# One core, attention and MLP of a decode step: three blocks of the output weights loaded mid-run in eight-row transfers, and w2 in four parts

## The chip, the cores and the metric

The kernel runs on one core of a Trainium2 chip. The metric is the time of one execution on the device in microseconds; the time before is 1313.02 us, the median of three runs (1312.48 to 1313.17). All arrays are float32.

## The reference

For eight tokens (B = 8, one position each, D = 512), with `xn = layernorm(x)`:

```
q  = (xn @ wq) as 32 heads of 128
k, v = the cached keys and values of 8 heads, 8192 positions, each serving 4 query heads
o  = softmax(q k^T / sqrt(128)) v                    (per token and head)
A  = o (8 x 4096) @ wo (4096 x 512)
h  = xn @ w1 + b1  (512 -> 1792);  act = h * tanh(softplus(h))
out = x + A + act @ w2  (1792 -> 512)
```

The caches are by far the largest part: 8 x 8 x 8192 x 128 numbers each for keys and values, 268 MB each. wq and wo have 8.4 MB each, w1 and w2 3.7 MB each.

## The kernel before

The host lays the arrays out so that every load is contiguous rows. The attention is worked through in 32 *units* j, each one token b = j % 8 and one pair m = j // 8 of key-value heads. A unit needs one key load and one value load, each 128 rows (partitions) of 64 KB, 8.39 MB (`load_unit`, L119 to L127).

One large buffer `kv` holds a value load and two key loads that overlap by half (L55 to L59). So a new key load can only be issued when the first half of the scores of the unit before has been computed (L446 to L450), and a new value load when the matmuls on the former one are done (L456 to L458). A second buffer `ws` takes a quarter of wq (2 MB) four times, each for the next eight units (L114 to L117). All these loads are issued on SyncE's queue (SP); x and b1 alone are loaded from ScalarE's queue (L132 and L134), x in 8 rows of 2 KB, b1 in 4 rows of 1792 B.

The schedule is written by hand: each engine runs the operations in the order of the program, and a framework adds the semaphores. A step of the loop (L441 to L472) for unit j is, in this order:

- `scores`: 32 products of the unit's keys with the spread queries into PSUM `S` (64 instructions, L279), with the issue of the next key load between the two halves.
- `softmax` (L289 to L313): maximum, transposed to and fro by TensorE, the exponential into the work tile `e` by ScalarE (L310).
- `values(j - 1)` (L337 to L354): 32 products of the *former* unit's weights with its values (64 instructions, L341), then four VectorE instructions that fold the result into `os` (L349, L351). After its matmuls the value load of unit j is issued.
- `key_weights(j + 1)` (two VectorE products, L262), and once in eight units `load_q`, `project` (products of wq on TensorE into PSUM `H`, copied into a tile that shares its name and buffers with `e`) and `spread`.
- `turn` (L315 to L334): TensorE permutes `e` into PSUM `X`, VectorE transposes and sums it into `pt8`, the weights of the next `values`.
- `merge(j - 1)` (L356 to L359): one product that turns `os`, scaled into `oT`, which holds the attention's result as 128 rows (position in the head) by head and token.

In the first unit `mish` computes the hidden layer and leaves its activations in `aT`. So w2's product could be done at any time; only its place in the buffer sets when w2 is loaded.

After the loop come the tail's loads (L475 to L487), all in `kv`: wo in four transfers of 2 MB (each with four *blocks* u of 128 rows by 4 KB), then w2 in three parts of 2, 1 and 0.5 MB. The tail's work in program order: `values` of the last unit, `outputs` (L409 to L419) for m = 0, 1, 2, eight products each, which accumulate o @ wo in PSUM `A` as four groups of partitions by head; `merge` of the last unit; `outputs` for m = 3; a copy of `A` by ScalarE (L495); `down` (L421 to L431) with w2's first part into PSUM `H`; four products with `bsel` that add the four groups of `A` into `H` (L497 to L504); `down` with the other parts; the addition of x by VectorE (L508) and the store (L509).

Of the kernel before, what the change touches and what calls it, by code (L numbers as in the profile page):

```python
# [8 lines left out]
F32 = mybir.dt.float32  # L9
# [4 lines left out]
P = 128  # L14
B = 8
D = 512
HKV = 8
REP = 4
DH = 128
# [8 lines left out]
BW = 1024  # L28
CC = D // P
# [3 lines left out]
Q = P // G  # L33
# [15 lines left out]
NJ = PL * HALF  # L49

W2R = 7

# [13 lines left out]
def kernel(  # L66
# [12 lines left out]
    nc = tc.nc  # L79
# [8 lines left out]
    ws = const.tile([P, CC * BW], F32, name="ws")  # L88
# [124 lines left out]
    def project():  # L213

        w = ws.rearrange("p (c f) -> p c f", c=CC)
        for d in range(2):
            for c in range(CC):
                nc.tensor.matmul(  # L218
                    H[Q * c : Q * c + B, :],
                    xn4[:, c, :],  # L220
                    w[:, c, d * 512 : (d + 1) * 512],
                    start=True,
                    stop=True,
                )
            qp = work.tile([P, 512], F32, name="e")
# [12 lines left out]
        return qT  # L238
# [50 lines left out]
    def softmax(j):  # L289
        nm = work.tile([P, 1], F32, name="nm")  # L290
        nc.vector.tensor_reduce(nm, S, axis=AX.X, op=ALU.max, negate=True)  # L291
        nc.tensor.transpose(M[:1, 0:P], nm, ident)  # L292
        nr = work.tile([1, 2, REP], F32, name="nr")
        row = M[:1, 0:P].rearrange("p (c d k h) -> p d h c k", c=2, d=2, h=REP)
        for d in range(2):
            nc.vector.tensor_reduce(nr[:, d], row[:, d], axis=AX.XY, op=ALU.min)
        nx = work.tile([1, 2, 2, NH * G, REP], F32, name="nx", bufs=1)
        for c in range(2):
            nc.vector.tensor_copy(  # L299
                nx[:, c],  # L300
                nr.rearrange("p d (o h) -> p d o h", o=1).to_broadcast([1, 2, NH * G, REP]),
            )
# [12 lines left out]
    def turn(j, lsel):  # L315
        e = E.pop(j)
        for g in range(4):
            nc.tensor.matmul(X[:, g], perm[:, g], e, start=True, stop=True)  # L318
        nc.tensor.matmul(M[:, 136 : 136 + H2], ones, lsel, start=True, stop=True)  # L319
        RT[j] = work.tile([P, H2], F32, name="rt", bufs=3)  # L320
        nc.vector.reciprocal(RT[j], M[:, 136 : 136 + H2])  # L321
        for tl in range(TL):
            nc.vector.transpose(  # L323
                tr.rearrange("p (l t) c -> p t l c", t=TL)[:, tl],
                X.rearrange("p g (t q l) -> p t l g q", t=TL, q=PP)[:, tl],
            )
        for d in range(2):
            half = slice(64 * d, 64 * (d + 1))
            nc.vector.tensor_reduce(  # L329
                pt8[half, :, :, d * REP : (d + 1) * REP].rearrange("p c y h -> p y c h"),  # L330
                tr[half].rearrange("p y (g c h) -> p y c h g", g=4, c=HALF),
                axis=AX.X,
                op=ALU.add,
            )  # L334


    def values(j, vt):  # L337
        for n in range(NJ):
            l, c = divmod(n, HALF)
            q = n % G  # L340
            nc.tensor.matmul(  # L341
                O[Q * q : Q * (q + 1), :],
                pt8[:, c, TL * l : TL * (l + 1), :].rearrange("p t h -> p (t h)"),
                vt[:, 512 * n : 512 * (n + 1)],
                start=(n < G),
                stop=(n >= NJ - G),
            )
        os = work.tile([P, DH], F32, name="os")
# [55 lines left out]
        nc.vector.tensor_copy(aT, turned.rearrange("p (j q) -> p j q", q=Q)[:, :, :B])  # L404


    A = X[:, 0]

    def outputs(m, t):  # L409
        w = t.rearrange("p (u f) -> p u f", u=4)  # L410
        for d in range(2):
            for h in range(REP):
                nc.tensor.matmul(
                    A[Q * h : Q * h + B, :],
                    oT[:, m, d * REP + h, :],
                    w[:, d * 2 + h // 2, h % 2 * D : (h % 2 + 1) * D],
                    start=(m == 0 and d == 0),
                    stop=(m == NP - 1 and d == 1),
                )  # L419

    def down(lo, hi, w):  # L421
        for j in range(2 * lo, 2 * hi):
            for g in range(G):
                at = (j - 2 * lo) * D + g * P
                nc.tensor.matmul(  # L425
                    H[Q * g : Q * g + B, :P],
                    aT[:, j, :],
                    w[:, at : at + P],
                    start=(j == 0),
                    stop=(j == 2 * W2R - 1),  # L430
                )  # L431

# [8 lines left out]
    for j in range(UNITS):  # L441
        b = j % B
        more = j // B + 1 < NP

        k = k_t.pop(j)
        scores(j, k, j % 2 == 1, 0)  # L446
        if j == UNITS - 1:
            v_t[j] = load_unit(v, j, K_AT[0])
        elif j > 0:
            k_t[j + 1] = load_unit(kT, j + 1, K_AT[(j + 1) % 2])  # L450
        scores(j, k, j % 2 == 0, 1)
        WK.pop(j)
        lsel = softmax(j)
        os = None
        if j > 0:
            os = values(j - 1, v_t.pop(j - 1))  # L456
        if j + 1 < UNITS:
            v_t[j] = load_unit(v, j, V_AT)  # L458
            if more and b == SPREAD_Q:
                spread(qT)  # L460
            key_weights(j + 1)
        if j == 0:
            mish(w1_t, b1_sb, kv[:, W1_AT : W1_AT + 6 * FG])
        if more and b == LOAD_Q:
            load_q(j // B + 1)
        if more and b == MAKE_Q:
            qT = project()
        turn(j, lsel)
        if j > 0:
            merge(j - 1, os)  # L470
        if more and b == SPREAD_Q - 1:
            selections()  # L472


    w_o = [kv[:, 4096 * m : 4096 * (m + 1)] for m in range(NP)]  # L475
    for m in range(NP):
        nc.sync.dma_start(
            w_o[m].rearrange("p (u f) -> p u f", u=4),
            wo[4 * m : 4 * (m + 1)].rearrange("u p f -> p u f"),
        )  # L480
    w2_rows = w2.rearrange("j p f -> (j p) f").rearrange("(q i) f -> q (i f)", i=W2R)
    w2_t = []
    parts = ((0, 4), (4, 6), (6, 7))
    for lo, hi in parts:
        t = kv[:, W2_AT + lo * BW : W2_AT + hi * BW]
        nc.sync.dma_start(t, w2_rows[:, lo * BW : hi * BW])
# [4 lines left out]
        outputs(m, w_o[m])  # L491
    merge(UNITS - 1, os)
    outputs(NP - 1, w_o[NP - 1])
    a_sb = work.tile([P, 512], F32, name="e")
    nc.scalar.copy(a_sb, A)  # L495
    down(*parts[0], w2_t[0])
    for g in range(G):  # L497
        nc.tensor.matmul(
            H[Q * g : Q * g + B, :P],
            bsel[:, :B],  # L500
            a_sb[:, g * P : (g + 1) * P],
            start=False,
            stop=False,
        )  # L504
    for p, t in zip(parts[1:], w2_t[1:]):
        down(*p, t)
    res = work.tile([P, DH], F32, name="os")
    nc.vector.tensor_add(res, H[:, :P], xres)  # L508
    nc.sync.dma_start(out, res)  # L509


# [36 lines left out]
```

## Time and profile before

| what | value |
|---|---|
| median of three runs | 1313.02 us (1312.48 to 1313.17) |
| the profiled execution, and its span | 1313.46 us, 1311.7 us |
| granted TensorE clock, mean | 0.877 |
| bytes read from HBM | 561.01 MB, 428 GB/s over the span |
| value loads, key loads | 32 each, median 30.1 and 29.9 us from issue to landing |
| wo transfers in the tail | 4 of 2048 KB, median 24.5 us to landing |
| w2 parts in the tail | 2048, 1024 and 512 KB; 35.4, 20.7 and 20.5 us to landing |

The span runs from the first to the last instruction; the execution's time is a little longer. "Share" of DMA is the mean busy share of the core's sixteen DMA engines; within short windows it can pass 1 by some per cent. In the rows of a window, each engine's busy time is followed by a count of instructions in brackets; the last three numbers are the granted TensorE clock, the DMA share and GB/s. A matmul on float32 shows as two instructions. "<-" in square brackets names what ended the engine's idle time.

### The profile page before, as it was taken

The page shows a single profiled execution, that of the slowest core. Times are in us where ns is not written, and L with a number is a line of the kernel's source. Part 1 is how long each engine was busy: PE and PEld are TensorE (multiplying, and loading weights), DVE is VectorE, ACT ScalarE, POOL GpSimd, SP SyncE. Part 2 cuts the span into 40 slices and gives each one's busy share as a digit, 9 for nine tenths or more (in the row PEclk, how much of TensorE's full clock was granted, in tenths as well). Part 3 has the DMA queues.
Part 4 walks back from the last instruction along what each step waited for, and adds up shares of the span by engine and source line. Part 5 has one row for each costly group of instructions (what it writes and reads, how often), then busy time and mean ns, then how long its engine had stood idle before and what let it go on. Part 6 is the DMA issues. An engine that isn't in the chain of part 4 may idle for free.

```text
span 1311.7 us, 11148 instructions
## 1 busy us (share of the span) xinstructions
PE 985.5 (75%) x5040; PEld 341.1 (26%) x5040; DVE 515.0 (39%) x728; ACT 40.2 (3%) x88; POOL 2.2 (0%) x9
## 2 busy tenths in 40 slices
PE   5968877768877668777878777687687678677666
PEld 3322222222322222222322222232232222222222
DVE  3463344432444442334243344414444432344431
ACT  1000000000000000000000000000000000000000
POOL 0000000000000000000000000000000000000000
PEclk9989888888888888887888788788898888888898
DMA  9999999999999999999999999999999999999997
GB/s 393 450 422 439 428 434 431 430 444 428 432 432 434 428 440 424 440 426 434 432 428 446 416 442 430 430 440 422 438 430 436 430 430 432 436 424 438 426 418 313
DMA packets 13591, 561.79 MB, mean 428 GB/s; under 512 B 1244, under 2 KB 1376, under 8 KB 4584
## 3 DMA queue, kind: packets, MB, share of 16 engines
q1 hardware_dynamic: 13520, 561.06, 99.2%
q8 instruction: 39, 0.64, 0.2%
q14 instruction: 8, 0.07, 0.0%
q10 hardware_dynamic: 24, 0.02, 0.0%
HBM read 561.01 MB, written 0.07 MB: 428 GB/s over the span
## 4 chain that ended last, share of the span: by engine, by line
DMA 73%; PE 23%; DVE 2%; issue 0%; ACT 0%; SPq 0%; DVEq 0%
DMA kv<-in_v 71%; PE o L341 20%; DMA kv<-in_w 3%; PE s L279 1%; DVE pt L329 1%; PE x L244 1%; PE h L425 0%; PE m L229 0%; PE h L218 0%; PE h L370 0%; DVE kv L392 0%; DVE tr L323 0%; DVE wk L262 0%; DVE nm L291 0%; ACT L177 0%
## 5 line engine op out<-in xcount | busy, mean ns | idle before, releaser
L279 PE MATMUL s<-kv,wk 128*64 128x512 f32 x2048 | 503.3, 654 | 179.3 <-DMA kv<-in_kT 175.4
L341 PE MATMUL o<-kv,pt 128*32 128x512 f32 x2048 | 269.9, 687 | 56.0 <-DMA kv<-in_v 46.4
L279 PEld LDWEIGHTS s<-kv,wk 128*64 128x64 f32 x2048 | 156.4, 151 | 500.9 <-issue 318.7
L329 DVE TENSOR_REDUCE pt<-tr 64x512 f32<-64x2048 f32 x64 | 241.3, 3770 | 1.6
L291 DVE TENSOR_REDUCE nm<-s 128x1 f32<-128x512 f32 x32 | 22.1, 691 | 369.2 <-PE s L279 369.2
L341 PEld LDWEIGHTS o<-kv,pt 128*32 128x32 f32 x2048 | 70.1, 124 | 229.4 <-issue 170.7
L318 PE MATMUL x<-e,perm 128*128 128x512 f32 x256 | 125.8, 636 | 2.0 <-ACT qr L251 2.0
L349 DVE TENSOR_SCALAR os<-o,isel 128x128 f32<-128x128 f32 x32 | 11.2, 351 | 277.3 <-PE o L341 277.3
L323 DVE STREAM_TRANSPOSE tr<-x 128x512 f32<-128x512 f32 x128 | 78.6, 671 | 0.0
L262 DVE TENSOR_TENSOR wk<-qr,mask 128x512 f32<-128x512 f32 x64 | 62.9, 1026 | 19.8 <-ACT qr L251 19.8
L318 PEld LDWEIGHTS x<-e,perm 128*128 128x128 f32 x256 | 49.0, 202 | 74.5 <-issue 72.0
L310 ACT ACTIVATE e<-s,nmx 128x512 f32<-128x512 f32 x32 | 22.0, 687 | 1097.4 <-DVE nmx L307 1097.4
L351 DVE SCALAR_TENSOR_TENSOR os<-o,isel,os 128x128 f32<-128x128 f32 x96 | 33.7, 351 | 3.4
L292 PE MATMUL m<-ident,nm 128*1 128x128 f32 x32 | 8.7, 273 | 28.8 <-DVE nm L291 28.8
L303 PE MATMUL m<-ident,nx 1*128 1x1 f32 x32 | 7.0, 219 | 24.2 <-DVE nx L299 24.2
L244 PE MATMUL x<-qT,tr 128*128 128x64 f32 x128 | 19.3, 315 | 3.0 <-ACT qr L251 2.7
L244 PEld LDWEIGHTS x<-qT,tr 128*128 128x128 f32 x128 | 18.1, 226 | 6.2 <-ACT qr L251 3.3
L321 DVE RECIPROCAL rt<-m 128x8 f32<-128x8 f32 x32 | 6.6, 207 | 33.4 <-PE m L319 33.4
L358 PE MATMUL m<-hsel,os 128*128 128x8 f32 x64 | 12.4, 266 | 9.3 <-DVE rt L321 9.3
L312 DVE TENSOR_SCALAR lsel<-rsel,l 128x8 f32<-128x8 f32 x32 | 7.4, 231 | 30.1 <-ACT e L310 30.1
L292 PEld LDWEIGHTS m<-ident,nm 128*1 128x1 f32 x32 | 2.5, 79 | 57.0 <-DVE nm L291 57.0
L319 PEld LDWEIGHTS m<-lsel,ones 128*128 128x128 f32 x64 | 12.2, 190 | 15.4 <-issue 15.2
(88 smaller groups left out, 163.7 us busy)
## 6 DMA issues: line engine op xcount, KB each, us to landing
ws<-in_wq SPq DMA_DIRECT2D x4, 2048.0 KB, 35.9
kv<-in_wo SPq DMA_DIRECT2D x4, 2048.0 KB, 24.5
kv<-in_w SPq DMA_DIRECT2D x1, 3584.0 KB, 26.7
kv<-in_w SPq DMA_DIRECT2D x1, 2048.0 KB, 35.4
kv<-in_w SPq DMA_DIRECT2D x1, 1024.0 KB, 20.7
kv<-in_kT SPq DMA_DIRECT2D x32, 29.9
kv<-in_v SPq DMA_DIRECT2D x32, 30.1
kv<-in_w SPq DMA_DIRECT2D x1, 512.0 KB, 20.5
```

Of the source, the lines that this page charges most:

```text
L244: nc.tensor.matmul(X[:, half, k * 64 : (k + 1) * 64], wide[:, half * 8 + k], qT, start=True, stop=True,)
L262: nc.vector.tensor_mul(w[:, :, d], q[:, :, d].to_broadcast([P, DI, NH * G, REP]), mask[:, d * NH * G : (d + 1) * NH * G] .rearrange("p (o ...
L279: nc.tensor.matmul(S[64 * c : 64 * (c + 1), :], w[:, i].rearrange("p d k h -> p (d k h)"), kk[:, i, c, :], start=(part == 0 and n == 0), s ...
L291: nc.vector.tensor_reduce(nm, S, axis=AX.X, op=ALU.max, negate=True)
L310: nc.scalar.activation(e, S, AF.Exp, bias=nmx, accum_out=l)
L318: nc.tensor.matmul(X[:, g], perm[:, g], e, start=True, stop=True)
L319: nc.tensor.matmul(M[:, 136 : 136 + H2], ones, lsel, start=True, stop=True)
L323: nc.vector.transpose(tr.rearrange("p (l t) c -> p t l c", t=TL)[:, tl], X.rearrange("p g (t q l) -> p t l g q", t=TL, q=PP)[:, tl],)
L329: nc.vector.tensor_reduce(pt8[half, :, :, d * REP : (d + 1) * REP].rearrange("p c y h -> p y c h"), tr[half].rearrange("p y (g c h) -> p y ...
L341: nc.tensor.matmul(O[Q * q : Q * (q + 1), :], pt8[:, c, TL * l : TL * (l + 1), :].rearrange("p t h -> p (t h)"), vt[:, 512 * n : 512 * (n ...
L351: nc.vector.scalar_tensor_tensor(os, O[:, DH * i : DH * (i + 1)], isel[:, i : i + 1], os, op0=ALU.mult, op1=ALU.add)
L358: nc.tensor.matmul(M[:, 168 : 168 + H2], os, hsel, start=True, stop=True)
```

## The change

Three edits, which belong together:

- **Three blocks of wo mid-run.** In units 22, 24 and 26, right behind the value load, one block of wo (block 0, 1 or 2; 512 KB) is loaded into `ws`, which wq no longer needs after unit 21. The block goes to partitions 0 to 31 as rows of 16 KB (four of its 128 rows side by side), in four transfers of eight partitions each: r, r + 4, ..., r + 28. In the following unit its eight products on 32 rows are added into PSUM `H` ahead of `turn`. For that, `turn_o` once brings the needed part of `oT` into the same order (four products with columns of the identity, one VectorE copy into `oX`). The tail's first transfer of wo has one block instead of four, and `outputs(0)` two products instead of eight.
- **w2 in four parts** of 1, 1, 1 and 0.5 MB in place of 2, 1 and 0.5.
- **The sum of wo ahead of w2.** wo's products accumulate in `H` through the run; in the tail the copy and the four `bsel` products come first, into PSUM `O`, and all of w2's products after them.

With these go: `project` stands behind `turn` instead of ahead of it, and the tiles `e` and `os` have one buffer each instead of two.

```diff
+FEW = 32
+LOAD_O = (22, 24, 26)
...
+    oX = const.tile([FEW, CC, 2 * len(LOAD_O) * B], F32, name="oX")
...
-        e = E[j] = work.tile([P, 512], F32, name="e")
+        e = E[j] = work.tile([P, 512], F32, name="e", bufs=1)
...
+    def load_o(u):
+
+        rows = wo[u].rearrange("(e r i) f -> r e (i f)", r=4, i=CC)
+        for r in range(4):
+            nc.sync.dma_start(ws[r:FEW:4], rows[r])
+
+    def turn_o():
+
+        n = 2 * len(LOAD_O) * B
+        o = oT[:, 0].rearrange("p h b -> p (h b)")[:, :n]
+        for i in range(CC):
+            nc.tensor.matmul(
+                M[:FEW, 256 + i * n : 256 + (i + 1) * n], ident[:, i::CC], o, start=True, stop=True
+            )
+        nc.vector.tensor_copy(oX.rearrange("p i n -> p (i n)"), M[:FEW, 256 : 256 + CC * n])
+
+    def early(u):
+        for n in range(2):
+            for i in range(CC):
+                nc.tensor.matmul(
+                    H[Q * i : Q * i + B, :],
+                    oX[:, i, (2 * u + n) * B : (2 * u + n + 1) * B],
+                    ws[:FEW, i * BW + n * D : i * BW + (n + 1) * D],
+                    start=(u == 0 and n == 0),
+                    stop=False,
+                )
...
+                u = d * 2 + h // 2
+                if m == 0 and u < len(LOAD_O):
+                    continue
                 nc.tensor.matmul(
-                    A[Q * h : Q * h + B, :],
+                    H[Q * h : Q * h + B, :],
...
+        if j in LOAD_O:
+            load_o(LOAD_O.index(j))
+        if j - 1 in LOAD_O:
+            if j - 1 == LOAD_O[0]:
+                turn_o()
+            early(LOAD_O.index(j - 1))
+        turn(j, lsel)
         if more and b == MAKE_Q:
             qT = project()
-        turn(j, lsel)
...
     for m in range(NP):
+        lo = len(LOAD_O) if m == 0 else 0
         nc.sync.dma_start(
-            w_o[m].rearrange("p (u f) -> p u f", u=4),
-            wo[4 * m : 4 * (m + 1)].rearrange("u p f -> p u f"),
+            w_o[m].rearrange("p (u f) -> p u f", u=4)[:, lo:],
+            wo[4 * m + lo : 4 * (m + 1)].rearrange("u p f -> p u f"),
         )
...
-    parts = ((0, 4), (4, 6), (6, 7))
+    parts = ((0, 2), (2, 4), (4, 6), (6, 7))
...
-    nc.scalar.copy(a_sb, A)
-    down(*parts[0], w2_t[0])
+    nc.scalar.copy(a_sb, H)
     for g in range(G):
         nc.tensor.matmul(
-            H[Q * g : Q * g + B, :P],
+            O[Q * g : Q * g + B, :P],
             bsel[:, :B],
             a_sb[:, g * P : (g + 1) * P],
-            start=False,
+            start=True,
             stop=False,
         )
-    for p, t in zip(parts[1:], w2_t[1:]):
+    for p, t in zip(parts, w2_t):
         down(*p, t)
```

More of the change, by code (lines that the diff above doesn't have):

```diff
@@ L224, in project @@
                 )
-            qp = work.tile([P, 512], F32, name="e")
+            qp = work.tile([P, 512], F32, name="e", bufs=1)
             nc.scalar.copy(qp, H)
@@ L347, in values @@
             )
-        os = work.tile([P, DH], F32, name="os")
+        os = work.tile([P, DH], F32, name="os", bufs=1)
         nc.vector.tensor_scalar(os, O[:, :DH], isel[:, 0:1], None, op0=ALU.mult)
@@ L404, in mish @@
         nc.vector.tensor_copy(aT, turned.rearrange("p (j q) -> p j q", q=Q)[:, :, :B])
-    A = X[:, 0]
+    def load_o(u):
[20 more added lines that the diff above has]
+                )
     def outputs(m, t):
@@ L412, in outputs @@
             for h in range(REP):
+                u = d * 2 + h // 2
+                if m == 0 and u < len(LOAD_O):
+                    continue
                 nc.tensor.matmul(
-                    A[Q * h : Q * h + B, :],
+                    H[Q * h : Q * h + B, :],
                     oT[:, m, d * REP + h, :],
-                    w[:, d * 2 + h // 2, h % 2 * D : (h % 2 + 1) * D],
-                    start=(m == 0 and d == 0),
+                    w[:, u, h % 2 * D : (h % 2 + 1) * D],
+                    start=False,
                     stop=(m == NP - 1 and d == 1),
@@ L425, in down @@
                 nc.tensor.matmul(
-                    H[Q * g : Q * g + B, :P],
+                    O[Q * g : Q * g + B, :P],
                     aT[:, j, :],
                     w[:, at : at + P],
-                    start=(j == 0),
+                    start=False,
                     stop=(j == 2 * W2R - 1),
@@ L493 @@
     outputs(NP - 1, w_o[NP - 1])
-    a_sb = work.tile([P, 512], F32, name="e")
-    nc.scalar.copy(a_sb, A)
-    down(*parts[0], w2_t[0])
+    a_sb = work.tile([P, 512], F32, name="e", bufs=1)
+    nc.scalar.copy(a_sb, H)
     for g in range(G):
         nc.tensor.matmul(
-            H[Q * g : Q * g + B, :P],
+            O[Q * g : Q * g + B, :P],
             bsel[:, :B],
             a_sb[:, g * P : (g + 1) * P],
-            start=False,
+            start=True,
             stop=False,
         )
-    for p, t in zip(parts[1:], w2_t[1:]):
+    for p, t in zip(parts, w2_t):
         down(*p, t)
-    res = work.tile([P, DH], F32, name="os")
-    nc.vector.tensor_add(res, H[:, :P], xres)
+    res = work.tile([P, DH], F32, name="os", bufs=1)
+    nc.vector.tensor_add(res, O[:, :P], xres)
     nc.sync.dma_start(out, res)
```

## The prediction

> **What bounds the kernel now.** I read the page first (busy shares, DMA queues, chain), then the chain of waits in order of time, then busy times in windows of a microsecond at the end, then the instructions there.
>
> ```profile
> PE 985.5 (75%) x5040; PEld 341.1 (26%) x5040; DVE 515.0 (39%) x728; ACT 40.2 (3%) x88; POOL 2.2 (0%) x9
> ...
> DMA  9999999999999999999999999999999999999997
> ...
> q1 hardware_dynamic: 13520, 561.06, 99.2%
> ...
> DMA 73%; PE 23%; DVE 2%; issue 0%; ACT 0%; SPq 0%; DVEq 0%
> ```
>
> No engine is full, but the sixteen DMA engines are: 99.2% of their time on one queue, above 90% in every slice but the last. The chain alternates between a value load and the matmuls after which the next may be issued.
>
> ```profile
> 956.74 29.83 DMA kv<-in_v
> 986.57 0.04 issue
> 986.61 8.81 PE o L341 x64
> 995.43 0.02 issue
> 995.45 29.83 DMA kv<-in_v
> ```
>
> ```profile
> 956.74:995.45 38.71, 31.35 (x175) 12.87 (x176) 15.38 (x21) 1.95 (x4) 0.00 (x0) 0.96 1.00 432
> ```
>
> In 38.71 us one key load and one value load pass, each of 128 rows of 64 KB (8.39 MB by the code): 16.78 MB, 433 GB/s, 27.1 GB/s per engine, DMA share 1.00. So the chain's "PE" parts aren't lost time: a key load moves meanwhile. What is ahead in the rings when a load is issued shows in the timeline:
>
> ```profile
> 974.39 0.33 SPq L123 DMA_DIRECT2D kv<-in_kT  x1
> ```
>
> ```profile
> 986.61 8.77 PE L341 MATMUL o<-kv,pt 128*32 128x512 f32 x64 [3.36 <-DMA kv<-in_v]
> ...
> 995.45 0.33 SPq L123 DMA_DIRECT2D kv<-in_v  x1
> ...
> 1005.97 4.53 PE L279 MATMUL s<-kv,wk 128*64 128x512 f32 x10 [6.14 <-DMA kv<-in_kT]
> ```
>
> At 974.39 the value load ahead was 12.2 us from landing (986.6); at 995.45 the key load ahead was 10.5 us from landing (1006.0). The rings don't run dry for engines less than about 10 us ahead of the last. So the time is bytes on the slowest DMA engine, plus what follows the last landing. That engines differ shows at the end (last two columns: DMA share, GB/s):
>
> ```profile
> 1299.00:1300.00 1.00, 1.00 (x12) 0.28 (x15) 0.00 (x0) 0.00 (x0) 0.00 (x0) 1.00 1.05 438
> 1301.00:1302.00 1.00, 0.00 (x0) 0.00 (x0) 0.00 (x0) 0.53 (x1) 0.00 (x0) 1.00 0.58 246
> 1302.00:1303.00 1.00, 0.00 (x0) 0.00 (x0) 0.00 (x0) 0.00 (x0) 0.00 (x0) 1.00 0.52 221
> 1303.00:1304.00 1.00, 0.28 (x12) 0.28 (x16) 0.00 (x0) 0.00 (x0) 0.00 (x0) 1.00 0.57 238
> 1305.00:1306.00 1.00, 1.00 (x28) 0.84 (x20) 0.00 (x0) 0.00 (x0) 0.00 (x0) 0.50 0.44 168
> 1306.00:1307.00 1.00, 1.00 (x28) 0.82 (x24) 0.00 (x0) 0.00 (x0) 0.00 (x0) 0.50 0.21 86
> ```
>
> All sixteen work to 1300; then the share is 0.52 to 0.58, which times 16 is 8.3 to 9.3 engines, so about nine; 0.44 is seven at 1305.5, and by 1307 all are done. Seven engines finish some 6.5 us ahead of the last ones, with equal shares of every large load.
>
> **The change part by part.** The profiled execution took 1313.46 us, its span 1311.7 (1.76 lie outside), 0.44 above the median of 1313.02 us. Sums are made against 1313.46.
>
> *Three blocks mid-run.* Bytes stay the same; their division need not. A block is 128 x 1024 x 4 B = 512 KB, now four transfers of eight rows of 16 KB. How many engines does an eight-row transfer use? Before has two short ones on queue 10: x (8 rows) and b1 (4 rows).
>
> ```profile
> q10 hardware_dynamic: 24, 0.02, 0.0%
> ```
>
> 24 packets are 8 rows + 8 completions and 4 rows + 4 completions: one engine a row. On sixteen engines x alone would show 16 completions. So I take eight engines, the same eight for all twelve transfers. Each gets 64 KB a block, at 27.1 GB/s 2.42 us, for three blocks 7.26 us. At the end each of the sixteen sheds 96 KB in 4 KB pieces:
>
> ```profile
> 1280.00:1300.00 20.00, 16.18 (x126) 4.20 (x130) 3.53 (x7) 0.00 (x0) 0.00 (x0) 0.82 1.03 416
> ```
>
> At 416/16 = 26.0 GB/s that is 3.78 us, at 27.1 it is 3.63; I take 3.7. The eight chosen end 3.55 us later than they did, the other eight 3.7 us earlier. About nine engines are late and eight are chosen: with nine late of sixteen, at least one of any eight is late. About six are busy after 1305.5, so the eight most likely hold one of the last. The last landing moves by **+3.55 us**. Bounds: nothing, if the transfers spread over sixteen; -3, if (against the count) no chosen engine is late; +3.7 at the top of the rates. A gap between small transfers in a ring is not shown: below it is bounded by zero (pieces queued back to back, share 1.00 across two loads' ends in the period above), above by the whole landing of a lone one:
>
> ```profile
> out<-os SPq DMA_DIRECT2D x1, 64.0 KB, 1.6
> ```
>
> 1.6 us less some 0.2 of data, twelve times, is 17 us. I take zero, by the row of a full queue, and leave 0.1 us each (1.2 in all) to the range.
>
> The Trainium skill, "DMA: Bandwidth & Descriptors", section "Rules for kernel authors", speaks against this edit: an outermost dimension below sixteen confines a transfer to as many engines, so put a multiple of sixteen there. The 24 packets agree; by the opposite reading (all sixteen share) the sum would be 3.55 us lower.
>
> *Issue and waits on SP.* The four issues stand behind the value load and ahead of the next key load, with the work buffer's last reader an iteration back; the next key load is issued some 18 us later anyway (974.39 to 995.45 is 21, 995.45 to the next the rest of 38.71), which hides some 1.5 us of issuing.
>
> *Matmuls mid-run.* Eight a block on 32 rows, once four more and a copy to turn the outputs, ahead of the transposition. Price by the like:
>
> ```profile
> 1291.31 5.32 PE L413 MATMUL x<-kv,oT 128*8 128x512 f32 x48
> ```
>
> Two rows are one product, so 24 take 5.32 us: eight cost 1.8 us (3.6 at half clock). At the first block PE also waits for the copy, which stands behind two products of this group on VectorE:
>
> ```profile
> L262 DVE TENSOR_TENSOR wk<-qr,mask 128x512 f32<-128x512 f32 x64 | 62.9, 1026 | 19.8 <-ACT qr L251 19.8
> ```
>
> That is 2 us, some 4 with the four products and the copy. PE was idle 6.14 us before its scores at 1005.97, which hides it; were the scores 3 us late, the key load would be issued 3 us late with 12 us still ahead of it. Without that cover each microsecond would cost one. The block lands 2.4 us after the value load issued just ahead of it, and its products stand behind 8.8 us of value matmuls: no wait. `project` behind the transposition, and single buffers for `e` and `os`: nothing, since by the order of the program their readers stand in the iteration that writes them, ahead of the scores that come before the next write.
>
> *The end.* Last landing and what follows it:
>
> ```profile
> L486 SPq DMA_DIRECT2D kv<-in_w x3: 963/1474/17052, 1268.3 to 1286.9; - x3
> ```
>
> ```profile
> kv<-in_w SPq DMA_DIRECT2D x1, 512.0 KB, 20.5
> ```
>
> ```profile
> 1298.93 1.47 PE L413 MATMUL x<-kv,oT 128*8 128x512 f32 x12 [1.98 <-DMA kv<-in_wo]
> ```
>
> ```profile
> 1296.99 0.17 DVE L359 TENSOR_TENSOR oT<-m,rt 128x8 f32<-128x8 f32 x1 [3.92 <-PE m L358]
> ```
>
> ```profile
> 1300.94 0.58 ACT L495 COPY e<-x 128x512 f32<-128x512 f32 x1 [42.72 <-PE x L413]
> 1303.72 3.26 PE L425 MATMUL h<-kv,aT 128*8 128x128 f32 x64 [2.88 <-DMA kv<-in_w]
> 1306.73 0.67 PE L498 MATMUL h<-e,bsel 128*8 128x128 f32 x8
> 1307.15 1.69 PE L425 MATMUL h<-kv,aT 128*8 128x128 f32 x48
> 1308.91 0.29 DVE L508 TENSOR_TENSOR os<-h,xres 128x128 f32<-128x128 f32 x1 [11.75 <-PE h L425]
> ```
>
> The last part of w2 lands at 1286.9 + 20.5 = 1307.4, and the final addition starts 1.5 us later, since PE had a backlog: it began at 1303.7 with 64 rows. In the new order wo's last products, the copy and the sums stand first, then four parts. Counting back from the last landing, by 224 KB of w2 per engine at 26.5 GB/s, wo's last block lands 8.7 us before it and the parts 6.2, 3.7, 1.2 and 0 us before it. The last value products are 7.26 us later than now (their loads are) and 6 of 24 products (1.3 us) are gone, so wo's last products, for which all but the landing stood ready at 1297.2, can start at 1297.2 + 7.26 - 1.3 = 1303.1 against a landing at 1298.9 + 3.55 = 1302.5: 0.6 late. With 1.8 of products (16 rows), 0.7 of copy and 0.6 of sums the first part starts 5.0 before the last landing. Each 1 MB part is 32 rows of 35 ns (1.69/48) to 51 ns (3.26/64), 1.1 to 1.6 us. The third starts at -1.2 and ends between -0.1 and +0.4; the last 16 rows end at +0.6 to +1.2. I take 1.0 in place of 1.5: **-0.5 us**; the ends are -0.9 and, if the products come later than that, +0.3.
>
> Sum: +3.55 - 0.5 = +3.05; 1313.46 + 3.05 = 1316.5 for an execution like the profiled one, less 0.44: **1316.1 us** as median.
>
> **The rivals.**
> 1. *Balance (the other side).* The eight chosen are all among those idle from 1300, and some load is taken off the late ones. They then end at 1300.5 + 3.55 = 1304.0, the others at 1306.9 - 3.7 = 1303.2; the last landing is 2.9 earlier, with the end's 0.5: 1313.0 - 3.4 = 1309.6. It decides as soon as no late engine is chosen. For it: seven idle engines are there to be used. Against it: seven are fewer than eight.
> 2. *The transfers use all sixteen*, so that the division doesn't change: 1313.0 - 0.5 = 1312.5. For it: every 128-row load uses sixteen. Against it: the 24 packets.
> 3. *Only the least late are chosen*, the two or three done by 1305.3: last landing 1305.3 + 3.55 = 1308.9 for 1306.9, less 0.5: 1314.5. Against it: six or seven of sixteen are later, and eight are drawn.
> 4. *Each small transfer stalls its rings*: 12 x 1.4 = 17 us more on the eight, 1333. For it: no short transfer mid-run is seen before. Against it: nothing stalls between the loads, and share 1.00. The Trainium skill, same page, section "Anatomy of one DMA — SWDGE (gpsimd) path", has a fixed cost of about 2.0 us a transfer, which it puts mostly on the confirmation of the last write; twelve of them in a row would be an estimate of 24 us, and the period of 38.71 us at full rate gives no sign that a queue with work waits for it.
>
> **How the numbers follow.** Forecast 0.73, rivals 1 to 4: 0.05, 0.10, 0.05, 0.07. The forecast's own range is 1315.3 to 1317.2 (landing +3.4 to +3.7, end -0.9 to +0.3, and 0.35 of scatter in the runs of before). The range takes in rival 3, and above the 1.2 us of small gaps: 1313.8 to 1318.0; rivals 1 and 2 and most of 4 stay out, 0.2 in all. 0.2%, about what a measurement of this kernel can tell from no change, is 2.6 us: 1310.4 to 1315.65. Faster: rival 1, 0.05. Same: rivals 2 and 3 and 0.10 of the forecast, 0.25. Slower: 0.63 of the forecast and rival 4, 0.70.
>
> **What would show it.** The eight rows: landing times of the value and key loads after units 22, 24 and 26 later by about 2.4 us each, and 7.3 later for the last value load; DMA share still near 1 on the way but below it, once early engines are more than 10 us ahead. The end: a tail of DMA share below one half that starts before 1300 and lasts to about 1310.5 instead of 1306.9. The order: the final addition 0.6 to 1.2 us after the last landing. I am wrong if the share drops to zero all at once (balance), if the last landing doesn't move (sixteen engines), or if the loads around the blocks slip by much over 2.4 us (stalls, or PE's scores late).

## The result and the profile after

The changed kernel takes 1317.05 us (median of seven runs, 1315.95 to 1317.75), the kernel before 1312.72 us beside it (seven runs, 1312.48 to 1313.27): a ratio of 1.0029, with a 95% interval of 1.002 to 1.0039. Another eight runs of the same kernel, in a later set, gave 1316.26 us (1315.84 to 1317.44), a ratio of 1.0026 (1.0016 to 1.0036). So it is slower by 3.1 to 4.3 us. Its profiled execution took 1316.37 us with a span of 1314.6, before 1313.46 and 1311.7.

The page of the changed kernel, with the lines that answer to those of before:

```profile
PE 997.1 (76%) x5084; PEld 341.5 (26%) x5084; DVE 515.3 (39%) x729; ACT 40.2 (3%) x88; POOL 2.2 (0%) x9
...
DMA  9999999999999999999999999999999999999997
...
q1 hardware_dynamic: 13472, 561.06, 99.1%
...
DMA 70%; PE 25%; DVE 3%; SPq 1%; ACT 0%; issue 0%; DVEq 0%; ACTq 0%
```

Almost nothing moves here. The bytes are the same 561.06 MB, the DMA engines are as full on average, and TensorE is busy 11.6 us longer without being the bound. A mean over sixteen engines can't show which of them is late.

The chain of waits of the changed kernel shows it; the columns are the start, the duration, and what it was:

```profile
997.33 30.28 DMA kv<-in_v
...
1036.13 32.63 DMA kv<-in_v
...
1078.89 28.60 DMA kv<-in_v
...
1114.67 33.95 DMA kv<-in_v
...
1233.18 32.61 DMA kv<-in_v
...
1291.35 19.50 DMA kv<-in_w
1310.86 0.04 issue
1310.90 0.67 PE o L459 x16
1311.57 0.02 issue
1311.59 0.29 DVE os L548
```

And the value loads of the same units in the chain of before:

```profile
1032.45 31.52 DMA kv<-in_v
1072.85 29.84 DMA kv<-in_v
1111.56 31.35 DMA kv<-in_v
...
1227.48 31.53 DMA kv<-in_v
```

Start and duration add to a landing. Behind the first block it is 1027.61 instead of 1025.28 (+2.3, the row of before is in the prediction); behind the second 1068.76 instead of 1063.97 (+4.8); behind the third 1148.62 instead of 1142.91 (+5.7); the last value load lands at 1265.84 instead of 1259.01 (+6.8). Three steps, one a block, the third complete only with the last load. The last landing of all is 1310.86 instead of 1307.4 (+3.46), and the final addition 1311.59 instead of 1308.91 (+2.68): at the end some 3.4 us were given back, and 0.8 more behind the last landing.

Windows at the end of the changed kernel (the last two columns are DMA share and GB/s):

```profile
1301.00:1302.00 1.00, 1.00 (x8) 0.09 (x2) 0.00 (x0) 0.00 (x0) 0.00 (x0) 1.00 1.02 422
1302.00:1304.00 2.00, 1.74 (x16) 0.63 (x18) 0.17 (x1) 0.00 (x0) 0.00 (x0) 1.00 0.79 317
1304.00:1306.00 2.00, 1.24 (x28) 0.51 (x24) 0.00 (x0) 0.59 (x1) 0.00 (x0) 1.00 0.27 113
1306.00:1307.00 1.00, 0.77 (x29) 0.48 (x20) 0.00 (x0) 0.00 (x0) 0.00 (x0) 1.00 0.21 90
1307.00:1308.00 1.00, 0.80 (x32) 0.77 (x32) 0.00 (x0) 0.00 (x0) 0.00 (x0) 1.00 0.17 70
1309.00:1310.00 1.00, 0.34 (x14) 0.34 (x18) 0.00 (x0) 0.00 (x0) 0.00 (x0) 1.00 0.11 45
```

Before, the share stood at 0.52 to 0.58 from 1301 to 1304: about nine engines. Now it is full to 1302, drops to 0.27 by 1306, and stays near 0.17 (times 16 is 2.7, about three engines) to 1308. The records of the DMA packets, which the trace keeps beside these views, give the ends one by one: eleven engines are done from 1303.0 to 1303.7, two at 1304.8, and the last three at 1308.5, 1309.9 and 1310.4. So thirteen are closer together than before, and three work alone for 4 to 6 us more. The three set the time.

The instructions of the changed kernel at the end:

```profile
1305.71 1.06 PE L459 MATMUL o<-kv,aT 128*8 128x128 f32 x32
1307.20 1.06 PE L459 MATMUL o<-kv,aT 128*8 128x128 f32 x32 [0.43 <-DMA kv<-in_w]
1309.66 1.06 PE L459 MATMUL o<-kv,aT 128*8 128x128 f32 x32 [1.40 <-DMA kv<-in_w]
1310.90 0.62 PE L459 MATMUL o<-kv,aT 128*8 128x128 f32 x16 [0.18 <-DMA kv<-in_w]
1311.59 0.29 DVE L548 TENSOR_TENSOR os<-o,xres 128x128 f32<-128x128 f32 x1 [8.82 <-PE o L459]
```

TensorE now waits for each of w2's parts but the first ("<-DMA"), where before it had a backlog; only the last part, sixteen instructions for eight products, stands behind the last landing.

### The profile page after: what moved, and what is told of

Its sections match the earlier page's. It is cut to its first block, busy times and chain, and to the rows that moved or that the text cites. A ratio compares the mean times of both kernels' runs of the same rounds, so it can differ in the third digit from the quotient of the medians.

```text
span 1314.6 us, 11261 instructions
## 1 busy us (share of the span) xinstructions
PE 997.1 (76%) x5084; PEld 341.5 (26%) x5084; DVE 515.3 (39%) x729; ACT 40.2 (3%) x88; POOL 2.2 (0%) x9
## 3 DMA queue, kind: packets, MB, share of 16 engines
q1 hardware_dynamic: 13472, 561.06, 99.1%
## 4 chain that ended last, share of the span: by engine, by line
DMA 70%; PE 25%; DVE 3%; SPq 1%; ACT 0%; issue 0%; DVEq 0%; ACTq 0%
DMA kv<-in_v 69%; PE o L347 20%; PE s L285 2%; DMA kv<-in_w 1%; SPq L527 1%; PE x L250 1%; DVE pt L335 1%; PE x L324 0%; PE h L376 0%; DVE wk L268 0%; PE m L235 0%; PE h L224 0%; PE h L432 0%; DVE kv L398 0%; DVE tr L329 0%
## 5 line engine op out<-in xcount | busy, mean ns | idle before, releaser
L285 PE MATMUL s<-kv,wk 128*64 128x512 f32 x2048 | 510.1, 662 | 167.1 <-DMA kv<-in_kT 164.4
L347 PE MATMUL o<-kv,pt 128*32 128x512 f32 x2048 | 266.5, 680 | 45.5 <-DMA kv<-in_v 35.9
L364 PEld LDWEIGHTS m<-hsel,os 128*128 128x128 f32 x64 | 10.1, 199 | 26.1 <-DVE qT L243 14.3
```

Of the source, the lines that this page charges most:

```text
L285: nc.tensor.matmul(S[64 * c : 64 * (c + 1), :], w[:, i].rearrange("p d k h -> p (d k h)"), kk[:, i, c, :], start=(part == 0 and n == 0), s ...
L347: nc.tensor.matmul(O[Q * q : Q * (q + 1), :], pt8[:, c, TL * l : TL * (l + 1), :].rearrange("p t h -> p (t h)"), vt[:, 512 * n : 512 * (n ...
L364: nc.tensor.matmul(M[:, 168 : 168 + H2], os, hsel, start=True, stop=True)
```

## The experiments

My theory was the prediction's: an eight-row transfer loads eight engines and no others, some of the eight are among the late ones, and everything else is hidden. The rivals: all sixteen engines share; each small transfer stalls its queue; the chosen ones are all early. Each diff below is against the changed kernel, and those of the extra loads behind the first show only the lines in which they differ from it. The kernel before ran beside each; its medians were 1313.07 to 1313.31 us.

**The tail alone.** No block mid-run; w2 in four parts and the sum of wo ahead stay.

```diff
-LOAD_O = (22, 24, 26)
+LOAD_O = ()
...
-                    start=False,
+                    start=(m == 0 and d == 0),
```

> Only the tail of the change: all of wo loaded in the tail as before, w2 in four parts, wo's sum ahead of all of w2's products. If the slowest DMA engine sets the time (theory), the last landing stays where it was and the final addition follows it 0.7 us later instead of 1.5: 0.8 us under before, some 1311.9. If the order of the tail is worth nothing (rival), 1312.7; if the change is slow because of its tail, 1315 or more.

Measured: 1312.59 us (11 runs, 1312.39 to 1313.1), ratio 0.9997 (0.9989 to 1.0006). Its last instructions:

```profile
1305.99 1.06 PE L458 MATMUL o<-kv,aT 128*8 128x128 f32 x32 [1.41 <-DMA kv<-in_w]
1307.23 0.62 PE L458 MATMUL o<-kv,aT 128*8 128x128 f32 x16 [0.18 <-DMA kv<-in_w]
1307.92 0.29 DVE L547 TENSOR_TENSOR os<-o,xres 128x128 f32<-128x128 f32 x1 [11.19 <-PE o L458]
```

The backlog is gone, and in the profile the final addition is 1.0 us earlier than in before. In the medians it is 0.5, inside the interval. So the tail's part of the change is worth about what the prediction gave it, and the 3 to 4 us of loss come from the blocks.

**The tail alone, w2 in three parts.** As above, with the former parts; it asks whether the fourth part or the order made the half microsecond.

```diff
-LOAD_O = (22, 24, 26)
+LOAD_O = ()
...
-                    start=False,
+                    start=(m == 0 and d == 0),
...
-    parts = ((0, 2), (2, 4), (4, 6), (6, 7))
+    parts = ((0, 4), (4, 6), (6, 7))
```

> The tail alone with w2 in three parts of 2, 1 and 0.5 MB again, wo's sum still ahead of them. By the spacing of the landings (3.7, 1.2 and 0 us before the last) 64 rows of 33 ns end 1.6 us before the last landing: nothing lost at full clock, 1312.6; at half clock 0.8 us more, 1313.4. If the four parts are what helps, 1313.1 or more in any case.

Measured: 1312.89 us (10 runs, 1312.36 to 1313.13), ratio 0.9996 (0.9987 to 1.0005). 0.3 us from four parts, no more than the scatter: which of the two edits gives the half microsecond can't be told.

**The same blocks over 128 partitions.** Each block goes mid-run in one transfer of 128 rows of 4 KB, so that the division among engines is that of every large load; its products need no turning, and are two a block.

```diff
-        rows = wo[u].rearrange("(e r i) f -> r e (i f)", r=4, i=CC)
-        for r in range(4):
-            nc.sync.dma_start(ws[r:FEW:4], rows[r])
+        nc.sync.dma_start(ws[:, u * BW : (u + 1) * BW], wo[u])
...
-            for i in range(CC):
...
+            h = (2 * u + n) % REP
+            nc.tensor.matmul(
+                H[Q * h : Q * h + B, :],
+                oT[:, 0, 2 * u + n, :],
+                ws[:, u * BW + n * D : u * BW + (n + 1) * D],
+                start=(u < 2),
+                stop=False,
+            )
...
-                turn_o()
```

> The change, but each of the three blocks is loaded mid-run by one transfer of 128 rows of 4 KB, so that all sixteen engines share it, and multiplied as it lies (two products a block, nothing to turn). Theory (eight rows, eight engines): the division among the engines is that of before, the time that of the tail alone, some 1311.9. Rival (a block moved mid-run costs by itself, by its issue, its waits or its products): 1315 or more, as with the change.

Measured: 1312.82 us (11 runs, 1312.61 to 1313.67), ratio 0.9999 (0.9991 to 1.0008). Its final addition:

```profile
1307.92 0.29 DVE L544 TENSOR_TENSOR os<-o,xres 128x128 f32<-128x128 f32 x1 [7.91 <-PE o L457]
```

The same instant as with the tail alone. Loading wo in the middle of the run costs nothing and gains nothing when all sixteen engines share it: what comes in addition mid-run is missing at the end. So the place isn't the cause; the eight rows are.

**The eight-row transfers as extra load.** The tail alone, and the change's twelve transfers beside it, with data that nobody uses; all of wo is still loaded in the tail. So what they cost is measured by itself, without what the end gives back.

```diff
-LOAD_O = (22, 24, 26)
+LOAD_O = ()
+EXTRA = (22, 24, 26)
...
-            nc.sync.dma_start(ws[r:FEW:4], rows[r])
+            nc.sync.dma_start(ws[r : 4 * 8 : 4], rows[r][:8])
...
-        if j in LOAD_O:
-            load_o(LOAD_O.index(j))
+        if j in EXTRA:
+            load_o(EXTRA.index(j))
```

> The tail alone, with all of wo in the tail, and on top the change's twelve eight-row transfers of 16 KB rows mid-run, whose data nobody reads: the price of these transfers by itself. Theory (one engine a row, some of the eight late already): 12 x 0.61 = 7.3 us over the tail alone, 1319.2. Rival (the load is shared by all sixteen engines): 1.57 MB at 433 GB/s, 3.6 us, 1315.5. Rival (small transfers stall their rings): 10 us or more, over 1322.

Measured: 1319.87 us (4 runs, 1319.79 to 1320.07), ratio 1.0052 (1.0038 to 1.0066). That is 7.28 us over the tail alone; the prediction gave the eight engines 7.26. It is also twelve times the 0.61 us that one piece takes in the trace's records of DMA packets (table below). If sixteen had shared, it would be half; if each transfer stalled by 1.4 us, it would be 17 more. Both rivals fall. With the 3.4 to 3.7 us that three blocks less are worth at the end, 1319.87 gives 1316.2 to 1316.5: the change's 1316.26, and about half a microsecond under its first 1317.05.

**Four, two and one rows.** The same, with fewer of the rows; each row is one piece of 16 KB on one engine, so each engine that is used gets the same 192 KB in all.

```diff
-            nc.sync.dma_start(ws[r:FEW:4], rows[r])
+            nc.sync.dma_start(ws[r : 4 * 4 : 4], rows[r][:4])
```

> As the former, but four rows of 16 KB a transfer, half the bytes, unused as well. Theory: four engines get 7.3 us more each. If one of these four is among the late ones, the time is again 7.3 us over the tail alone, 1319.2, though the bytes are half; if none is, they have some 6.5 us in hand and the time rises by 1 us at most, 1312.9. Rival (bytes over all engines): 1.8 us, 1313.7.

```diff
-            nc.sync.dma_start(ws[r:FEW:4], rows[r])
+            nc.sync.dma_start(ws[r : 4 * 2 : 4], rows[r][:2])
```

> As the former two, with two rows of 16 KB a transfer, a quarter of the bytes, unused. With four rows one engine of the lowest four was late at the end. Theory: if it is one of the lowest two, the time is the same 5.6 us over the tail alone, 1318.2; if not, both have about 6.5 us in hand against 7.3 and the time rises by 1 us at most, 1313.4. Rival (bytes over all engines): 0.9 us, 1313.5.

```diff
-            nc.sync.dma_start(ws[r:FEW:4], rows[r])
+            nc.sync.dma_start(ws[r : 4 * 1 : 4], rows[r][:1])
```

> One row of 16 KB a transfer, unused. Theory: one engine gets 7.3 us more; 1318.2 if it is the late one, 1313.4 at most if it is an early one. Rival (a single row is cut and shared by all sixteen): 0.5 us, 1313.0.

Measured: four rows 1318.22 us (4 runs, 1317.98 to 1318.35), ratio 1.0039 (1.0023 to 1.0054); two rows 1313.02 (9 runs, 1312.74 to 1313.12), ratio 1.0 (0.999 to 1.0009); one row 1312.76 (9 runs, 1312.61 to 1312.98), ratio 0.9998 (0.9988 to 1.0007). Over the tail alone: +7.3, +5.6, +0.4 and +0.2 us for eight, four, two and one row. Half the bytes cost three quarters of the time, a quarter of them almost nothing. That isn't a cost by bytes but by engines: which ones are chosen decides. It isn't a cost by transfers either, since each of the four runs issues twelve. The end with four rows, in windows (DMA share in the column before the last):

```profile
1308.00:1310.00 2.00, 1.15 (x44) 0.86 (x37) 0.00 (x0) 0.00 (x0) 0.00 (x0) 1.00 0.10 37
1310.00:1312.00 2.00, 0.65 (x26) 0.36 (x20) 0.00 (x0) 0.00 (x0) 0.00 (x0) 1.00 0.06 25
```

0.06 times 16 is one engine, which works alone from 1310 to 1312. Its last packet ends at 1312.4; less the 7.3 us it would have ended at 1305.1, among the engines that are neither first nor last in the kernel before. So four rows meet the premise of the prediction's third rival, the least late engine, which fits 5.6 us instead of 7.3. The packet records say the same from the other side: a piece starts when its engine has finished what is ahead in its ring. In the change, 20 of a block's 32 pieces (five engines) start within 2.7 us of the first, and 12 (three engines) 4 us or more after it; with four rows it is 12 and 4 (three engines early, one late); with two rows all 8 start early. The two engines that two rows use are early ones, done 6.2 to 6.9 us before the last in the kernel before; 7.3 us more makes them the last by 0.4 to 1.1, and 0.4 was measured. That is the premise of the prediction's rival of balance, early engines that take more for almost nothing, met in two engines and not in eight.

The Trainium skill, "DMA: Bandwidth & Descriptors", section "Why a DMA increments its semaphore by 16 and not by 1", has the rule behind this: a transfer issued this way uses the largest number of engines up to sixteen that divides the slowest dimension on both sides, and always the lowest-numbered of them. The pieces agree with the first half: eight, four and two engines. With the second they only go together, since no packet's record names its engine: the one late engine among the four isn't among the two.

**The blocks two units later.** Rival: the rings run dry for some engines in unit 23, where the turning of `oT` and the spreading of the queries meet.

```diff
-LOAD_O = (22, 24, 26)
+LOAD_O = (24, 26, 28)
```

> The change with its blocks two units later (24, 26 and 28), so that the first products don't fall into the unit that also spreads the queries, where the scores started 7 us later than before. Theory (slowest DMA engine alone): the time of the change, 1316.4 to 1317.1. Rival (the late scores of that unit let the rings run dry in some executions): 0.7 us less and less scatter, 1316.3.

Measured: 1316.55 us (8 runs, 1315.98 to 1317.62), ratio 1.0027 (1.0017 to 1.0037), against 1316.26 for the change in the same set. No difference: the place in the run isn't the cause. The timeline of the changed kernel, from the first block's products in unit 23 to the scores of unit 24, shows what was hidden there:

```profile
960.88 0.68 PE L424 MATMUL m<-oT,ident 128*32 128x48 f32 x8
...
963.84 3.60 PE L432 MATMUL h<-ws,oX 32*8 32x512 f32 x16 [2.28 <-DVE oX L427]
967.37 6.17 PE L324 MATMUL x<-e,perm 128*128 128x512 f32 x8
...
974.27 10.95 PE L285 MATMUL s<-kv,wk 128*64 128x512 f32 x50
...
981.40 0.33 SPq L129 DMA_DIRECT2D kv<-in_kT  x1
```

The scores start at 974.27, and the timeline of the kernel before has their first row at 967.27:

```profile
967.27 9.23 PE L279 MATMUL s<-kv,wk 128*64 128x512 f32 x42 [0.80 <-DMA kv<-in_kT]
```

They are 7 us late, and the next key load is issued 7 us late, at 981.40 instead of 974.39. Not all of it was covered: by the packet records two engines had nothing to do from 979.7 and 979.8 on, and up to five at once, until the packets of that key load began at 982.4. They were engines that were ahead, so it cost nothing: the next value load of the chain still lands only the 2.3 us late that the first block accounts for.

**The change again.** The same file, in the same set as the runs with two rows, one row and the later units.

> The change itself, beside the others on the same chip, since its seven runs scatter by 1.8 us and those of the extra transfers by 0.3. If the tail alone (1312.6) plus twelve transfers (7.3) less what the tail sheds (3.4 to 3.7) is all, 1316.2 to 1316.5; if something mid-run adds to it, 1317.0 again.

Measured: 1316.26 us (8 runs, 1315.84 to 1317.44), ratio 1.0026 (1.0016 to 1.0036). So of the first 1317.05, about 0.8 is scatter between sets of runs; the fifteen runs lie between 1315.84 and 1317.75.

**Two rows that are used.** If two engines are early, they should take a load that is of use: the first head's half of block 0 (256 KB) in sixteen transfers of two rows, four in each of four units, its four products after the last of them; the tail's first transfer of wo is shorter by as much.

```diff
-LOAD_O = (22, 24, 26)
+LOAD_O = (22, 24, 26, 28)
...
-        rows = wo[u].rearrange("(e r i) f -> r e (i f)", r=4, i=CC)
-        for r in range(4):
-            nc.sync.dma_start(ws[r:FEW:4], rows[r])
+        rows = wo[0].rearrange("(e r i) f -> r e i f", r=16, i=CC)[..., :D]
+        for r in range(4 * u, 4 * (u + 1)):
+            nc.sync.dma_start(
+                ws[r:FEW:16, : CC * D].rearrange("p (i f) -> p i f", i=CC), rows[r]
+            )
...
```

> The change with its transfers turned to the engines that have time in hand: the lowest two took 7.3 us more each at a price of 0.4 us in all. In place of three blocks only the first head's half of block 0 (256 KB) goes mid-run, in sixteen transfers of two rows, and the tail's first transfer is shorter by it. Theory: the two engines get 4.8 us more and shed 0.6, within their 6.5; all others shed 0.6; 0.6 under the tail alone, 1312.0. Rival (a block mid-run costs by its products and waits): at or over the tail alone, 1312.6 to 1313.5.

Measured: 1315.99 us (11 runs, 1315.75 to 1316.21), ratio 1.0022 (1.0013 to 1.003): a miss, 4 us over the expectation and 3.4 over the tail alone. Its final addition:

```profile
1311.46 0.29 DVE L550 TENSOR_TENSOR os<-o,xres 128x128 f32<-128x128 f32 x1 [10.70 <-PE o L460]
```

One thing that I had left out shows in the packet records: the 64 pieces of 2 KB that each of the two engines gets take 8.3 us in all and not 4.8, at 0.08 us a piece for about half of them, as for the 2 KB pieces of the tail, and about 0.16 for the others. That is 7.7 us net, a little over what they had in hand, and doesn't make up 3.4. Another is where the rows go: with stride 16, to partitions r and r + 16 for r from 0 to 15, and no longer to every fourth one. The two runs that follow test whether that matters, with other shapes; how the 3.4 us of this run divide between the two isn't shown.

**Sixteen rows of 8 KB as extra load.** As the eight-row extra load, with the same bytes and all sixteen engines: rows to partitions r, r + 4, ..., r + 60.

```diff
-        rows = wo[u].rearrange("(e r i) f -> r e (i f)", r=4, i=CC)
+        rows = wo[u].rearrange("(e r i) f -> r e (i f)", r=4, i=2)
...
-            nc.sync.dma_start(ws[r:FEW:4], rows[r])
+            nc.sync.dma_start(ws[r : 4 * 16 : 4, : 2 * BW], rows[r])
```

> The twelve unused transfers of the eight-row run with the same bytes, as 16 rows of 8 KB each. Theory (one engine a row): sixteen engines get 96 KB more each, 3.6 us, half of what eight rows cost; 1316.2. Rival (the price hangs on the number of transfers or on the bytes, however divided): 7.3 us, 1319.9.

Measured: 1326.11 us (3 runs, 1325.5 to 1326.46), ratio 1.0097 (1.0082 to 1.0113). A miss on both sides: twice the engines, half the bytes on each, and 6.2 us *more* than eight rows. What is new beside the number of engines and the size of the rows is where the second half of the rows goes: to partitions 32 to 63.

**Eight rows side by side.** The eight-row extra load with nothing changed but the partitions: eight consecutive ones instead of every fourth.

```diff
-            nc.sync.dma_start(ws[r:FEW:4], rows[r])
+            nc.sync.dma_start(ws[8 * r : 8 * (r + 1)], rows[r])
```

> The twelve unused eight-row transfers once more, with the same rows, bytes and partitions 0 to 31, but each transfer goes to eight partitions side by side (0 to 7, 8 to 15, ...) instead of every fourth one (r, r + 4, ...). Why: 16 rows to every fourth partition from 0 to 63, and two rows sixteen partitions apart, cost more than the engines' division explains, and their pieces took twice as long beside other loads. Theory (a group of four partitions is one engine's in every large load; a piece that another engine writes there waits its turn, and the owner too): four engines now meet in one group, pieces of 2 us and more for 0.61, and the time is 1330 or more. Rival (only the rows of a transfer count, not where they go): 1319.9, as with every fourth partition.

Measured: 1336.74 us (4 runs, 1332.77 to 1338.95), ratio 1.0174 (1.0152 to 1.0196): 17 us over the same bytes, rows and instructions at every fourth partition. So where the rows go counts, and the theory's time is met; its pieces are not, at 1.06 us and not 2 or more (table below). One window around the first block, for eight rows at every fourth partition:

```profile
930.00:970.00 40.00, 33.66 (x176) 13.57 (x174) 9.46 (x20) 1.95 (x4) 0.00 (x0) 0.90 1.01 436
```

for sixteen rows:

```profile
930.00:970.00 40.00, 33.82 (x170) 13.12 (x166) 8.84 (x16) 1.95 (x4) 0.00 (x0) 0.83 1.01 399
```

and for eight rows side by side:

```profile
930.00:970.00 40.00, 32.74 (x166) 12.65 (x163) 8.53 (x16) 1.95 (x4) 0.00 (x0) 0.80 1.00 389
```

The DMA share is about 1.00 in all three, and the rate 436, 399 and 389 GB/s: an engine whose packets are slowed still counts as busy. The records of the packets show it one by one (median and longest in us; the last columns count the large loads' 64 KB packets, within 12 us of the blocks, that took over 2.57 us, and sum what these took above the usual 2.418):

```
                     piece  count  median  longest   slow 64 KB packets   excess, us
the change           16 KB     96    0.61     0.62        3 of 588             1.5
extra, 8 rows        16 KB     96    0.61     0.62        5 of 613             2.4
extra, 4 rows        16 KB     48    0.61     0.62        7 of 594             4.5
extra, 2 rows        16 KB     24    0.61     0.62        3 of 520             1.5
two rows, used        2 KB    128    0.12     0.19       41 of 728            17.6
extra, 16 rows        8 KB    192    0.56     0.68      137 of 591           108.7
side by side         16 KB     96    1.06     1.62      187 of 607           169.3
```

In the first four rows the pieces take 0.61 us and hardly a large packet is slowed. In the last three both slow down, the pieces (8 KB take 0.31 us in the tail, 2 KB 0.08) and some of the large packets. The Trainium skill, "SBUF — State Buffer", section "Door 1: The DMA port swizzle (why `[64,N]` ≈ `[32,N]`)", gives a likely reason: four neighbouring partitions share one of sixteen ports, partitions 0 to 63 reach eight of them, and in a load of 128 partitions each engine serves one port. In the first four rows of the table each engine then writes the port that it serves anyway, if row e goes to engine e; eight rows side by side are two ports for eight engines, and sixteen rows at stride four are eight ports for sixteen. The order of the three rates agrees. That the ports are the cause is argued: the runs with eight rows show that the partitions decide, and the packets' records name neither engine nor port.

## Why the prediction came out right, by its steps

- **Eight engines, +7.26 us.** Right. 7.28 by the extra load alone, +6.8 in the profile's last value load. The three landings moved in three steps. The count of 24 packets on a small queue was enough to tell it.
- **At least one late engine among the eight.** Right in what it says, and it decided the sign, by a count only (nine late of sixteen). Which ones, it couldn't say: three of the nine late ones were in the eight, beside five of the seven early ones. With four or two rows in place of eight the same argument would have given no answer, and the runs show the least late engine and the early ones instead.
- **Shed at the end, −3.7 us, net +3.55.** Right: +3.46 for the last landing. From the extra load to the change it is −3.6 in the medians (1319.87 to 1316.26).
- **No gap between small transfers.** Right: 0.61 us a piece, back to back, twelve of them 7.3. The fixed 2.0 us a transfer that the Trainium skill, "DMA: Bandwidth & Descriptors", section "Anatomy of one DMA — SWDGE (gpsimd) path", gives for transfers issued from GpSimd isn't to be seen here, with transfers from SP behind a full ring.
- **Issue on SP.** Right in the outcome: the four issues took 2.7 to 2.8 us and not 1.5, and the key load behind the first block still went out at 936.92, against 937.42 before.
- **Mid-run work hidden.** Right in the outcome, too small in the size: the scores of unit 24 were 7 us late and not 3. TensorE waited 2.28 us for the copy, the products took 3.60 at a granted clock of 0.50, and the transposition of `e` behind them took 6.17 at 0.59 instead of 3.70 at 1.00. The prediction named the half clock for the products and not for what follows them. The 12 us that were still ahead in the rings covered 7 for the late engines, which set the time; some of the early ones ran dry.
- **The end, −0.5 us.** −0.8 in the profile (0.7 from landing to addition instead of 1.5), −0.5 in the medians of the tail alone. Within its bounds of −0.9 and +0.3.
- **What the end looks like.** Partly wrong. I wrote of a DMA share below one half from before 1300; it was full to 1302 and below one half only from about 1304. The prediction's own numbers would have said so: the late engines that aren't chosen end 3.7 us earlier, at 1303.2, and the early chosen ones at 1304.0, where eleven engines did end. The last packet ended at 1310.4, as expected.
- **What was missing.** The 2.42 us a block hold only for the partitions that the stride of four gives. The prediction took this price without asking where the rows go, and that was luck; side by side the unused load cost 17 us more.

The gain that the change might have had went nowhere: what is taken off the end is taken off all sixteen engines alike, and of the eight that get more mid-run three were already late. No version here clearly beats the kernel before: the tail alone, at 1312.59, is inside the interval. Whether one or two rows of *useful* data, with the stride of four, would gain from the 6.5 us in which early engines stand idle wasn't tried. Also open is why the medians of the same kernel differed by 0.8 us between two sets.

## What to carry to other kernels

When the DMA engines are the bound, count bytes by engine, not in sum: look for a DMA share between 0 and 1 at the end of the run, and ask of each transfer with fewer than sixteen rows which engines it uses and whether they are the late ones. Ask also to which partitions its rows go: here every fourth one cost 17 us less than neighbours. And don't trust a share of 1.00 without the GB/s beside it. An unused extra transfer, run by itself on top of the kernel, prices such an edit more cleanly than the edit does.

## What the runs showed of the hardware that I had not expected

- The partitions to which a small transfer goes can slow both it and the large loads beside it: to eight neighbouring ones, 16 KB took 1.06 us at the median and up to 1.62 instead of 0.61, and 187 of 607 large packets were stretched, 169 us in sum over the engines.
- A one-row transfer of 16 KB stayed on one engine: four pieces a block, back to back, and +0.2 us in all.
- The engines of the kernel before may end as far apart as they do because of instruction fetches, which the same engines carry. This is the row of the changed kernel's page (packets, MB, share), and the page of before has the same:

```profile
q8 instruction: 39, 0.64, 0.2%
```

  Of these 39 packets of 16 KB each delays its engine by 1.55 us, as far as the packets behind it show. The engines of before end in three groups, at 1300.0 to 1300.7 (seven), 1304.7 to 1304.9 (three) and 1306.4 to 1306.9 (six): the second and third are about three and four such delays behind the first. No experiment took the fetches away, so this is argued and not shown.
